# Normalising the probabilities before their transposes, and converting weights in steps of 512 columns, in a fused top-k attention and rational FFN kernel

## The chip, the cores and the metric

The kernel runs on one core of one Trainium2 chip. The core has five engines that work from queues of their own: TensorE (PE in the profile, with its weight loads shown apart as PEld), VectorE (DVE), ScalarE (ACT), GpSimd (POOL) and SyncE (SP), which here only issues transfers. Each engine executes its instructions in the order in which they stand in its queue, and waits on semaphores for the others. The metric is the device time of one execution in microseconds (us), as a median over runs.

## The reference

Eight batches of eight heads with 576 positions of 64 numbers go through attention that keeps the 32 largest scores of each row. Its output, 4608 tokens of 512 numbers, goes through an FFN whose activation is a ratio of two polynomials.

```python
scores = scale * np.matmul(q, k.transpose(0, 1, 3, 2))
kth = np.partition(scores, -top_k, axis=-1)[..., -top_k:-top_k + 1]
scores = np.where(scores >= kth, scores, -1000000000.0)
attn = np.exp(scores - np.max(scores, axis=-1, keepdims=True))
attn = attn / (np.sum(attn, axis=-1, keepdims=True) + 1e-09)
x = np.matmul(attn, v)        # then laid out as 4608 x 512
...
h = x @ w_in
P = a[0] + a[1] * h + a[2] * h2 + a[3] * h3
Q = 1.0 + np.abs(b[0]) * np.abs(h) + np.abs(b[1]) * h2
g = P / (Q + 1e-06)
return (g @ w_out).astype(np.float32)
```

The weights `w_in` (512 x 2048) and `w_out` (2048 x 512) arrive as 64-bit floats and are turned into 32-bit ones on the chip.

## The kernel before

A **tile** is 128 queries of one head against all 576 keys; there are 288, counted with the tiles of the last 64 queries, for which two heads share one tile (such a unit is called `mixed`). Two tiles, the two heads `h` of a head pair `hp`, make a **unit** (160 of them, 32 of which are mixed). Four head pairs times two units of queries fill a **chunk** of 256 tokens, and there are 18 chunks.

One tile (`add_tile`) goes through these steps. PE computes the scores `s` into PSUM. ACT copies them to `sb`. DVE folds the two halves of a row into `hi` and `lo`, and then finds the 32nd largest by MAX8 and MATCH_REPLACE8 in turns (tiles `m`, `hi`, `lo`). ACT makes the exponentials `e`, for which POOL or ACT has scaled the row's largest score to `st`. DVE multiplies `e` by the mask into `pr` and adds up the row into `ss` (L791). `pr` has two buffers of one unit each.

One unit (`add_values`) then goes on: POOL or ACT adds 1e-9 to the sums (`guard`), DVE takes the reciprocal (`inverse`, L846), and ACT widens the reciprocals of both heads to a 128 x 128 tile `rw` (`widen`, L285). PE transposes the probabilities in three parts, 4, 4 and 1 blocks of 128 columns, into PSUM tiles `trp` (L868), and with the third part also `rw` (L870). ACT copies each part to `p` (L880); the third part has 256 columns, half of them the transposed reciprocals. After both units of a pair PE multiplies `p` by the values into `av` (L894), ACT copies `av` to the chunk's tile `x` or `xm` (L911, L921), and POOL multiplies that by the transposed reciprocals (L913, L925). So the division by the sum stands at the end, on 64 output columns per head.

The **FFN** of a chunk works in 8 groups of 256 hidden columns (`add_group`). PE computes `ph` in 24 matmuls (L1041, three products of a split into high and low parts). ACT computes three functions of `ph`, POOL the cubic (L1115, L1116), ACT three functions more, POOL the ratio (L1097), its rounded part `g` (L281) and the rest `gl` (L1103), and PE adds the group's share into `po` in 12 matmuls (L1187). There are 144 groups. The working tiles of a group are taken from a pool `t` of 14 tiles of 512 columns. The PSUM tag `mm` with two banks is shared by `trp`, `ph` and `av`.

**Weights** are converted in the first 200 us, in 32 blocks of 128 x 512 and each block in two steps of 256 columns: two functions on ACT (L416, L421), a merge on DVE (L427), one more function on ACT (L433) and a product on POOL (L437).

The **order** is made at build time by `Plan`. Each step has a key, a list of engines that may run it, and modelled lengths; a list scheduler walks through a modelled time, and on a free engine starts the ready step with the lowest key whose buffers are free. What it decides is written out as the fixed order of each engine's queue. The numbers of the keys are in `KEY`. `STAY` is taken off the key of a PE step of the kind (ordinary or rounded 32-bit operands) that PE has just run; before it is 0. At the end of the program PE writes one row `flag_row` that DVE reduces (L1337), which decides whether a second, exact version of the program is run; in the profiled execution it isn't.

## Time and profile before

| | us |
|---|---|
| median of 3 runs | 1486.34 |
| lowest and highest | 1482.77 and 1486.7 |
| the profiled execution, its own time | 1483.46 |
| span of that execution, first to last instruction | 1481.4 |

The profile gives for each engine the time in which it was busy, groups of equal instructions with the mean length of one, and the waits with what ended them. A recorded length reaches from the start of an instruction to its end; on PE, DVE and ACT the next instruction often starts before that end, so the price of one instruction in a row of others is read from start to start. The profiled execution's span leaves 2.1 us of its own time outside, and its own time is 2.9 us under the median.

### The profile page before, as it was taken

The page shows a single profiled execution, that of the slowest core. Times are in us where ns is not written, and L with a number is a line of the kernel's source. Part 1 is how long each engine was busy: PE and PEld are TensorE (multiplying, and loading weights), DVE is VectorE, ACT ScalarE, POOL GpSimd, SP SyncE. Part 2 cuts the span into 40 slices and gives each one's busy share as a digit, 9 for nine tenths or more (in the row PEclk, how much of TensorE's full clock was granted, in tenths as well). Part 3 has the DMA queues.
Part 4 walks back from the last instruction along what each step waited for, and adds up shares of the span by engine and source line. Part 5 has one row for each costly group of instructions (what it writes and reads, how often), then busy time and mean ns, then how long its engine had stood idle before and what let it go on. Part 6 is the DMA issues. An engine that isn't in the chain of part 4 may idle for free.

```text
span 1481.4 us, 32234 instructions
## 1 busy us (share of the span) xinstructions
PE 1388.4 (94%) x9729; PEld 1178.2 (80%) x9729; DVE 1353.0 (91%) x4567; ACT 1297.7 (88%) x2616; POOL 1183.8 (80%) x1756
## 2 busy tenths in 40 slices
PE   5566689999999999999999999999999999999998
PEld 3335568888887888888888888888888788888896
DVE  7999999999999999999999999999999999999100
ACT  7888889989897898999899989999898798999774
POOL 5987897789776796879777887788777696887896
PEclk9766899999999999999999999999999999999999
DMA  7887876567765767577766776567665767554564
GB/s 238 266 248 229 245 213 193 184 199 229 225 193 147 242 203 223 174 213 228 224 181 198 219 246 186 183 198 230 212 192 157 246 187 223 177 183 142 172 197 139
DMA packets 172744, 302.94 MB, mean 204 GB/s; under 512 B 24209, under 2 KB 77969, under 8 KB 172561
## 3 DMA queue, kind: packets, MB, share of 16 engines
q1 hardware_dynamic: 172560, 300.79, 66.5%
q8 instruction: 79, 1.29, 0.4%
q14 instruction: 105, 0.85, 0.2%
HBM read 229.94 MB, written 18.87 MB: 168 GB/s over the span
## 4 chain that ended last, share of the span: by engine, by line
PE 80%; DVE 6%; ACT 5%; POOL 4%; DMA 2%; issue 2%; SPq 1%; POOLq 0%; DVEq 0%; ACTq 0%
PE ph_m L1041 23%; PE po_m L1187 21%; PE av L894 10%; PE s L720 8%; PE trp L868 8%; PE ph_t L1041 3%; PE po_t L1187 3%; DVE m L749 2%; DVE hi L757 2%; PE s L711 2%; ACT p L880 1%; DVE pr L791 1%; PE trp L870 1%; ACT sb L727 1%; POOL cf L484 1%
## 5 line engine op out<-in xcount | busy, mean ns | idle before, releaser
L749 DVE MAX8 m<-hi 128x8 f32<-128x288 f32 (+1 forms) x1152 | 498.6, 453 | 0.2
L757 DVE MATCH_REPLACE8 hi<-m,hi 128x288 f32<-128x288 f32 x864 | 380.8, 445 | 0.0
L1041 PE MATMUL ph_m<-xh_m,win_h 128*128 128x256 f32 x1024 | 304.4, 297 | 6.6 <-DMA win_l<-w_w 2.7
L1041 PE MATMUL ph_m<-xh_m,wi_m 128*128 128x256 f32 x1024 | 290.8, 284 | 0.6 <-DMA wi_m<-win_l 0.5
L1041 PE MATMUL ph_m<-xl_m,win_h 128*128 128x256 f32 x1024 | 289.9, 283 | 0.0
L880 ACT COPY p<-trp 128x512 f32<-128x512 f32 (+1 forms) x448 | 226.9, 513 | 31.7 <-PE trp L868 22.7
L868 PE MATMUL trp<-ident,pr 128*128 128x128 f32 x1312 | 222.3, 282 | 27.3 <-ACT p L880 16.0
L791 DVE SCALAR_TENSOR_TENSOR pr<-sb,m,e 128x576 f32<-128x576 f32 x288 | 230.3, 800 | 1.3 <-ACT e L788 0.9
L1097 POOL TENSOR_TENSOR pa_m<-pa_m,va_m 128x512 f32<-128x512 f32 x128 | 165.4, 1292 | 78.4 <-ACT va_m L1094 76.3
L727 ACT COPY sb<-s 128x576 f32<-128x576 f32 x288 | 184.4, 640 | 49.7 <-PE s L720 35.0
L788 ACT ACTIVATE e<-sb,st 128x576 f32<-128x576 f32 x288 | 217.0, 754 | 12.2 <-DVE pr L791 7.6
L1187 PE MATMUL po_m<-wout,g_m 128*128 128x512 f32 x512 | 217.9, 426 | 0.4 <-POOL fl L774 0.4
L868 PEld LDWEIGHTS trp<-ident,pr 128*128 128x128 f32 x1312 | 165.3, 145 | 56.8 <-ACT p L880 17.9
L1041 PEld LDWEIGHTS ph_m<-xh_m,win_h 128*128 128x128 f32 x1024 | 195.0, 190 | 15.6 <-ACT p L880 4.2
L1187 PE MATMUL po_m<-wl_m,g_m 128*128 128x512 f32 x512 | 203.0, 397 | 1.9 <-DMA wl_m<-wout_l 1.8
L1187 PE MATMUL po_m<-wout,gl_m 128*128 128x512 f32 x512 | 202.5, 396 | 0.1
L1041 PEld LDWEIGHTS ph_m<-xl_m,win_h 128*128 128x128 f32 x1024 | 195.3, 191 | 2.6
L1041 PEld LDWEIGHTS ph_m<-xh_m,wi_m 128*128 128x128 f32 x1024 | 194.6, 190 | 1.1 <-DMA wi_m<-win_l 1.0
L894 PE MATMUL av<-p,vm 128*64 128x256 f32 (+1 forms) x1920 | 186.7, 343 | 4.0 <-ACT p L880 3.8
L1116 POOL TENSOR_TENSOR pa_m<-pa_m,hh_m 128x512 f32<-128x512 f32 x128 | 165.3, 1291 | 16.0 <-ACT hh_m L1122 6.3
L1103 POOL TENSOR_TENSOR gl_m<-pa_m,g_m 128x512 fp32r<-128x512 f32 x128 | 165.8, 1295 | 6.8 <-PE po_t L1187 0.3
L894 PEld LDWEIGHTS av<-p,vm 128*64 128x64 f32 x1920 | 111.7, 142 | 72.3 <-issue 15.4
(121 smaller groups left out, 3204.4 us busy)
## 6 DMA issues: line engine op xcount, KB each, us to landing
wi_m<-win_l SPq DMA_DIRECT2D x128, 512.0 KB, 3.8
wl_m<-wout_l SPq DMA_DIRECT2D x256, 256.0 KB, 3.2
q<-qx SPq DMA_DIRECT2D x252, 128.0 KB, 2.7
vm<-in_v_dram SPq DMA_DIRECT2D x96, 320.0 KB, 3.1
km<-in_qk_dram SPq DMA_DIRECT2D x32, 352.0 KB, 3.6
kl<-in_qk_dram SPq DMA_DIRECT2D x32, 288.0 KB, 4.0
w_w<-in_moe_w_in_dram SPq DMA_DIRECT2D x32, 256.0 KB, 5.1
w_w<-in_moe_w_out_dram SPq DMA_DIRECT2D x32, 256.0 KB, 3.6
```

The lines of the kernel that those rows point to most:

```text
L727: nc.scalar.copy(t.sb, t.s[:, :, 0:HF])
L749: nc.vector.max(to, t.both if not full and o == 24 else getattr(t, src))
L757: nc.vector.match_replace(x, t.m[:, o : o + 8], x, NEG)
L788: nc.scalar.activation(t.e, t.sb, AF.Exp, scale=SCALE, bias=t.st)
L791: nc.vector.scalar_tensor_tensor(out=t.pr, in0=t.sb, scalar=t.kth, in1=t.e, op0=ALU.is_ge, op1=ALU.mult, accum_out=u.ss[:, t.h : t.h + 1],)
L868: nc.tensor.transpose(u.ps[i][:, c * P : (c + 1) * P], u.pr[:, x], ident)
L880: nc.scalar.copy(pair.pT[i][:, at].rearrange("p c n -> p (c n)"), u.ps[i][:, 0 : n * P])
L894: nc.tensor.matmul(pair.av[d, 0 : u.nq * len(pair.units)], lhs, x[:, 0, d] if u.mixed else x[:, 0] if lone else x, start=(c == 0), stop=(c ...
L1041: nc.tensor.matmul(y.ph[:, f * NT : (f + 1) * NT], w, z[:, c, :], start=(c == 0 and i == 0), stop=(c == HP - 1 and i == 2),)
L1097: engine().tensor_tensor(out=y.pa, in0=y.pa, in1=y.va, op=ALU.mult)
L1103: engine().tensor_tensor(out=tile_("gl", F32R), in0=y.pa, in1=y.g.bitcast(F32), op=ALU.subtract)
L1187: nc.tensor.matmul(o.po[i], z, w, start=(ff == 0 and n == 0), stop=(ff == NF - 1 and n == 2),)
```

## The change

Three things change, and the planner's numbers with them.

1. **The division moves.** `widen`, the transpose of `rw` and the two products on POOL after `av` are gone. In their place a step `normal(h)` for each of the unit's tiles multiplies the 576 probabilities of a row in `pr` by the reciprocal, on POOL or ACT as the planner finds (172 stand on POOL and 116 on ACT in the built order). The transposes now wait for these products and no longer for L791 alone. The third part of `p` has 128 columns in place of 256. ACT's copy of `av` into `x` or `xm` is now the last step.
2. **Weight conversion in one step of 512 columns** for each block: one load, and each of the five operations once per block in place of twice. A variant on DVE alone that was not in use is dropped.
3. **Working tiles of the FFN.** The pool of 14 tiles `t` becomes 4 tiles `t` and 5 tiles `tt` of double width; `hh` and `va` share one `tt`, `g` and `gl` another. The rounding of `g` (`RH`) may run on ACT as well as on POOL; 46 of 144 stand on ACT.

In the planner, a PE step of the kind that PE has just run has 10 or 15 taken off its key, and 14 of the other numbers in `KEY` differ (among them `MOE` and `PACE`, which place the FFN's steps among the tiles', from 125.2 to 157.9 and from 17.4 to 19.1, and `EX` for the exponentials from 14.4 to 25.7).

```diff
-        items = sorted(ready, key=lambda i: (i[0] - KEY['STAY'] * self.stays(e, i[2]), i[1]))
+        stay = KEY['STF'] if self.kind == "f" else KEY['STR']
+        items = sorted(ready, key=lambda i: (i[0] - stay * self.stays(e, i[2]), i[1]))
...
-            s1 = add("ACT", act_sb(256), sign, [ld], key + 1)
...
+            s1 = add("ACT", act_sb(512), sign, [ld], key + 1)
+            s2 = add("ACT", act(512, 1) + 0.04, ends, [ld], key + 1, take=[bits_hold])
+            s3 = add("DVE", 0.65, merge, [s1, s2], key + 1, later=KEY['ML'])
+            s4 = add("ACT", act_sb(512), size, [s3], key + 2, give=[bits_hold])
+            last = [add("POOL", pool_t(512), join, [s4], key + 2, give=hold if plain else [])]
...
-        def widen():
-            u.rw = buf("rw", [P, 2, D], F32, f"rw_{u.nm}")
-            ss = u.ss[:, 0:nr].unsqueeze(2)
-            scaled(u.rw, ss.broadcast_to([P, 2, D]), 1.0)
+        def normal(h):
+            def emit():
+                x = u.pr[:, h * S : (h + 1) * S]
+                scaled(x, x, u.ss[:, h : h + 1])
+            return emit
...
-                if i == 2:
-                    nc.tensor.transpose(
-                        u.ps[i][:, P : 2 * P], u.rw.rearrange("p h d -> p (h d)"), ident
-                    )
...
-                n = NJ if i < 2 else 2
+                n = NJ if i < 2 else 1
...
-        rw = add(one(P, 0, KEY['WD']), None, widen, [inv, prev.rw], key + KEY['URG'], take=[rwhold], give=[u.uhold])
+        norm = [
+            add({**one(S, 1, KEY['NR']), "POOL": 0.74} if "POOL" in KEY['NR'] else one(S, 1, KEY['NR']),
+                None, normal(h), [inv], key + KEY['URG'] + h, give=[u.uhold])
+            for h in range(nr)
+        ]
...
-            dep = [t1]
-            if i == 2:
-                dep += [rw, dbl]
+            dep = norm[0:1] if i == 0 else norm[1:2] if i == 1 else norm + [dbl]
...
-            c = add("ACT", act(n), lambda: scale(1), [m2] + u.chunk.parts[0:1], key + KEY['URG'], give=[avh])
-            u.done = add("POOL", pool_t(n), lambda: scale(2), [c], key + KEY['URG'], give=[thold[2]])
+            u.done = add("ACT", act(n), scale, [m2] + u.chunk.parts[0:1], key + KEY['URG'], give=[avh])
...
-        mm, th = Hold("mm"), {n: Hold("t") for n in ("h", "va", "hh", "pa", "g", "gl")}
+        mm, th = Hold("mm"), {n: Hold(t) for n, t in (("hv", "tt"), ("pa", "t"), ("gg", "tt"), ("h", "t"))}
```

The order of the queues shows the change at two places. The first is on PE in the middle of the program, where the third part of one unit's transposes stands (`trp_4_3_1`, from `pr_3_1`; `po` are matmuls of the FFN, `av` the product with the values, `s` the scores). Before:

```order
L1187 MATMUL po_m_2_1_12665<-wout_87,g_m_2_3_12625 128x512
L1187 MATMUL po_m_2_1_12665<-wout_87,gl_m_2_3_12643 128x512
L1187 MATMUL po_m_2_1_12665<-wl_m_2_3_1_12976,g_m_2_3_12625 128x512
L868 MATMUL trp_4_3_1_13114<-ident,pr_3_1_12895 128x128
L870 MATMUL trp_4_3_1_13114<-ident,rw_3_1_13106 128x128
L1187 MATMUL po_m_2_0_12654<-wout_88,g_m_2_4_12780 128x512
L1187 MATMUL po_m_2_0_12654<-wout_88,gl_m_2_4_12809 128x512
L1187 MATMUL po_m_2_0_12654<-wl_m_2_4_0_12994,g_m_2_4_12780 128x512
L894 MATMUL av_3_1_13132<-p_4_2_1_12911,vm_1_2_12564 64x256
```

Now:

```order
L1121 MATMUL po_m_2_0_11981<-wout_89,gg_m_2_4_12320 128x512 x2
L1121 MATMUL po_m_2_0_11981<-wl_m_2_4_1_12377,gg_m_2_4_12320 128x512
L818 MATMUL trp_4_3_1_12535<-ident,pr_3_1_12358 128x128 x4
L669 MATMUL s_3_2_1_12546<-kb_2_9920,q_2_2_11968 128x288 x4
L818 MATMUL trp_4_3_1_12556<-ident,pr_3_1_12358 128x128
L1121 MATMUL po_m_2_1_11990<-wout_89,gg_m_2_4_12320 128x512 x2
L1121 MATMUL po_m_2_1_11990<-wl_m_2_4_1_12377,gg_m_2_4_12320 128x512
L1121 MATMUL po_m_2_0_11981<-wout_90,gg_m_2_5_12457 128x512 x2
```

The transpose of `rw` has gone, the second and the third part have moved apart by one tile's scores, and the rest of the row is as it was.

The second is on POOL in the middle of the program (`fl` is a check of the 32 largest, `ss` the sums, `pa`, `g`, `gl`, `gg` and `hv` the FFN's, `st` the scaled largest score, `x_m` the chunk). Before:

```order
L281 TENSOR_SCALAR g_m_0_4_11682<-pa_m_0_4_11542 128x512
L774 TENSOR_TENSOR fl_10990<-hi_0_1_11483,m_0_1_11507 128x2
L1103 TENSOR_TENSOR gl_m_0_4_11691<-pa_m_0_4_11542,g_m_0_4_11682 128x512
L281 TENSOR_SCALAR ss_0_1_11570<-ss_0_1_11570 128x2
L913 TENSOR_TENSOR x_m_0_11702<-x_m_0_11702,p_4_0_0_11510 128x256
L1115 TENSOR_SCALAR pa_m_0_5_11680<-pa_m_0_5_11680,cf 128x512
L1116 TENSOR_TENSOR pa_m_0_5_11680<-pa_m_0_5_11680,hh_m_0_5_11687 128x512
L1097 TENSOR_TENSOR pa_m_0_5_11680<-pa_m_0_5_11680,va_m_0_5_11697 128x512
```

Now:

```order
L282 TENSOR_SCALAR ss_4_3_10656<-ss_4_3_10656 128x1
L282 TENSOR_SCALAR gg_m_0_1_10713<-pa_m_0_1_10509 128x512
L288 TENSOR_SCALAR st_0_0_10630<-m_0_0_10629 128x1
L1037 TENSOR_TENSOR gg_m_0_1_10713<-pa_m_0_1_10509,gg_m_0_1_10713 128x512
L288 TENSOR_SCALAR pr_4_3_10655<-pr_4_3_10655,ss_4_3_10656 128x576
L804 TENSOR_SCALAR pr_4_3_10655<-pr_4_3_10655 128x64
L1049 TENSOR_SCALAR pa_m_0_2_10785<-pa_m_0_2_10785,cf 128x512
L1050 TENSOR_TENSOR pa_m_0_2_10785<-pa_m_0_2_10785,hv_m_0_2_10798 128x512
L282 TENSOR_SCALAR ss_0_0_10738<-ss_0_0_10738 128x2
L723 TENSOR_TENSOR fl_10438<-hi_0_0_10572,m_0_0_10629 128x2
L288 TENSOR_SCALAR pr_0_0_10737<-pr_0_0_10737,ss_0_0_10738 128x576
```

The product on `x_m` has gone, and the products on `pr` with 576 columns now stand between the FFN's products. Of the 172 on POOL, 89 stand directly behind a product of two tensors of 512 columns or more. Of the 116 on ACT, 19 stand directly ahead of a copy of scores to `sb`.

In the whole order, 384 matmuls `ph` and 243 matmuls `po` stood behind the last scores on PE before; now 384 and 228 do.

## Rows read from the trace of the kernel before

**Rows 1.** The page: busy time by engine; then DVE in 40 slices of the span.

```profile
PE 1388.4 (94%) x9729; PEld 1178.2 (80%) x9729; DVE 1353.0 (91%) x4567; ACT 1297.7 (88%) x2616; POOL 1183.8 (80%) x1756
...
DVE  7999999999999999999999999999999999999100
```

**Rows 2.** Busy time in three stretches: PE, PEld, DVE, ACT, POOL, PE's clock, DMA.

```profile
0.00:300.00 300.00, 222.05 (x1377) 173.70 (x1378) 285.40 (x959) 261.28 (x600) 242.60 (x416) 0.86 0.74 226
300.00:1376.00 1076.00, 1068.23 (x7754) 918.27 (x7753) 1066.89 (x3605) 970.07 (x1908) 857.39 (x1260) 1.00 0.66 202
1376.00:1481.00 105.00, 98.12 (x602) 86.26 (x600) 0.69 (x5) 66.37 (x110) 83.85 (x82) 0.98 0.54 169
```

**Rows 3.** Waits of DVE: total us, times, longest.

```profile
DVE again L1337 <- PE flag_row L1335: 97.9, 1, 97.9
DVE hi L738 <- ACT sb L727: 12.5, 12, 7.2
```

**Rows 4.** Timeline of PE near 804 us: start, length.

```profile
804.35 0.27 PE L868 MATMUL trp<-ident,pr 128*128 128x128 f32 x1
804.46 0.27 PE L870 MATMUL trp<-ident,rw 128*128 128x128 f32 x1
```

**Rows 5.** The chain that ended last: start, length, what, count.

```profile
1412.19 6.98 PE po_m L1187 x30
...
1443.17 2.88 PE ph_m L1041 x24
```

**Rows 6.** Groups by form on PE: count, busy us, mean ns, idle before.

```profile
L870 PE MATMUL trp<-ident,rw 128*128 128x128 f32 x160 | 44.8, 280 | 6.5 <-ACT rw L285 5.6 <-DMA w_w<-in_moe_w_out_dram 0.9
```

**Rows 7.** Groups by form on ACT.

```profile
L788 ACT ACTIVATE e<-sb,st 128x576 f32<-128x576 f32 x288 | 217.0, 754 | 12.2 <-DVE pr L791 7.6 <-POOL st L287 2.3 <-POOL qx L281 1.0
...
L880 ACT COPY p<-trp 128x512 f32<-128x512 f32 x288 | 166.7, 587 | 23.8 <-PE trp L868 22.7
...
L880 ACT COPY p<-trp 128x256 f32<-128x256 f32 x160 | 60.8, 380 | 7.9 <-PE trp L870 6.5 <-POOL xm L925 0.7
L285 ACT ACTIVATE rw<-ss 128x128 f32<-128x128 f32 x160 | 50.5, 315 | 5.4 <-DVE ss L846 4.5 <-PE trp L870 0.3
L421 ACT ACTIVATE w_w_b<-w_w,toggle 128x256 f32<-128x256 uint32 x64 | 31.4, 503 | 0.3
...
L279 ACT ACTIVATE kh<-kl 128x576 fp32r<-128x576 f32 x5 | 3.4, 677 | 0.0
```

**Rows 8.** Groups by form on POOL.

```profile
L1097 POOL TENSOR_TENSOR pa_m<-pa_m,va_m 128x512 f32<-128x512 f32 x128 | 165.4, 1292 | 78.4 <-ACT va_m L1094 76.3
...
L281 POOL TENSOR_SCALAR g_m<-pa_m 128x512 fp32r<-128x512 f32 x128 | 79.5, 621 | 6.3
L913 POOL TENSOR_TENSOR x_m<-x_m,p 128x256 f32<-128x256 f32 x64 | 47.3, 739 | 7.5 <-ACT x_m L911 7.4
...
L925 POOL TENSOR_TENSOR xm<-xm,p 64x64 f32<-64x64 f32 x64 | 20.4, 319 | 12.8 <-ACT xm L921 9.6 <-DVE pr L791 0.5
...
L281 POOL TENSOR_SCALAR kh<-kl 128x576 fp32r<-128x576 f32 x27 | 18.2, 674 | 3.0 <-DMA kl<-in_qk_dram 1.7 <-issue 1.0
```

**Rows 9.** Timeline of DVE near 167 us, a step of weight conversion.

```profile
167.02 0.43 DVE L427 SCALAR_TENSOR_TENSOR w_w_b<-w_w,w_w_b 128x256 int32<-128x256 int32 x1 [0.75 <-ACT w_w_b L421]
167.35 0.08 DVE L757 MATCH_VALUE_LOAD hi<-m,hi 128x8 f32 x1
167.43 0.44 DVE L757 MATCH_REPLACE8 hi<-m,hi 128x288 f32<-128x288 f32 x1
167.79 0.45 DVE L738 TENSOR_TENSOR hi<-s,sb 128x288 f32<-128x288 f32 x1
```

**Rows 10.** Timeline of DVE near the last units.

```profile
1366.92 0.80 DVE L791 SCALAR_TENSOR_TENSOR pr<-sb,m,e 128x576 f32<-128x576 f32 x1
...
1370.31 0.16 DVE L846 RECIPROCAL ss<-ss 128x2 f32<-128x2 f32 x1
```

**Rows 11.** Timeline of PE at the same place.

```profile
1368.03 0.60 PE L868 MATMUL trp<-ident,pr 128*128 128x128 f32 x4
```

More of the change, by code (lines that the diff above doesn't have):

```diff
@@ L361, in load @@
             def load():
-                o.raw = []
-                for i, e in enumerate(range(0, 512, 256)):
-                    x = words(i)
-                    if i == 0:
-                        o.first = x
-                    r = x.bitcast(I32)
-                    nc.sync.dma_start(r, rows[:, e : e + 256].bitcast(I32))
-                    r = r.rearrange("p (e t) -> p e t", t=2)
-                    o.raw.append((slice(e, e + 256), r[:, :, 0], r[:, :, 1], x[:, 0:256]))
-                o.w = hi if plain else words(2)
@@ new lines, in load, with place_bits @@
+                o.first = words(0)
+                r = o.first.bitcast(I32)
+                nc.sync.dma_start(r, rows.bitcast(I32))
+                r = r.rearrange("p (e t) -> p e t", t=2)
+                o.raw = r[:, :, 0], r[:, :, 1]
+                o.w = hi if plain else words(1)[:, 0:512]
+                o.low = o.first[:, 0:512].bitcast(F32R) if away is not None else lo
+            ld = add("SP", dma(1, P * 1024), load, key=key, take=hold)
+            bits_hold = Hold(bank_tag)
+            def place_bits():
+                o.bits = bank(bits_hold, [P, 512], f"w_{nm}_b").bitcast(I32)
+                return o.bits
@@ new lines, in sign, with ends, merge, size @@
+            def sign():
+                nc.scalar.activation(o.w, o.raw[1].bitcast(F32), AF.Sign)
+            def ends():
+                nc.scalar.activation(
+                    place_bits().bitcast(F32), o.raw[0].bitcast(U32), AF.Identity, scale=THREE, bias=toggle
+                )
+            def merge():
+                nc.vector.scalar_tensor_tensor(
+                    o.bits, o.raw[1], 3, o.bits, op0=ALU.logical_shift_left, op1=ALU.bitwise_xor
+                )
+            def size():
+                nc.scalar.activation(o.first[:, 0:512], o.bits.bitcast(F32), AF.Abs)
@@ L899, in multiply, with scale @@
             return emit
-        def scale(part=0):
+        def scale():
             x = u.chunk
@@ L909, in scale @@
                 av = pair.av[:, 0 : n * P].rearrange("p (j n) -> p j n", j=n)
-                if part == 1:
-                    nc.scalar.copy(y, av)
-                elif part == 2:
-                    nc.gpsimd.tensor_tensor(out=y, in0=y, in1=rb[:, 0:n], op=ALU.mult)
-                else:
-                    nc.vector.tensor_tensor(y, av, rb[:, 0:n], ALU.mult)
+                nc.scalar.copy(y, av)
                 return
@@ L918, in scale @@
                 u.batch.xm = buf("xm", [P, HP, TAIL], F32, f"xm_{u.bi}")
-            y = u.batch.xm[:, u.hp]
-            if part == 1:
-                nc.scalar.copy(y, pair.av[:, 0:TAIL])
-                return
-            for h in range(2):
-                d = slice(h * D, (h + 1) * D)
-                nc.gpsimd.tensor_tensor(out=y[d], in0=y[d], in1=rb[d, 0, d], op=ALU.mult)
+            nc.scalar.copy(u.batch.xm[:, u.hp], pair.av[:, 0:TAIL])
         def put():
@@ L1128, in add_group @@
         wdep = []
-        held = [th[n] for n in (("hh", "va", "pa", "h") if full else ("hh", "va", "pa"))]
+        held = [th[n] for n in (("hv", "pa", "h") if full else ("hv", "pa"))]
         early = not full and x.n < KEY['TN']
@@ L1163, in add_group @@
         l2 = add("ACT", act_sb(512), inverse, [l1], k2 + 0.7)
-        gg = add(two(512, *KEY['ratio']), None, ratio, [l2, s3], k2 + 0.8, give=[th["va"]])
-        used = [th["g"], th["gl"]] if split_g else [th["pa"]]
+        gg = add(two(512, *KEY['ratio']), None, ratio, [l2, s3], k2 + 0.8, give=[th["hv"]])
+        used = [th["gg"]] if split_g else [th["pa"]]
         for h in used:
@@ L1168, in add_group @@
         if split_g:
-            gg = add(one(512, 0, KEY['RH']), None, ratio_high, [gg], k2 + 0.8, take=[th["g"]])
+            gg = add(one(512, 0, KEY['RH']), None, ratio_high, [gg], k2 + 0.8, take=[th["gg"]])
             gg = add(two(512, *KEY['ratio_low']), None, ratio_low, [gg], k2 + 0.8,
-                     take=[th["gl"]], give=[th["pa"]])
+                     give=[th["pa"]])
         def project(f, i):
```

119 lines of the change are left out of this document (28 added, 91 removed).

## The prediction, made before the changed kernel was run

> **What bounds the kernel now.** I read four views, in this order.
>
> First the busy time by engine and the slices [rows 1]. PE is the fullest engine, with 94% of the span, and DVE has 91%. But the slices of DVE show how its share comes about: it is full from the first slice on and stops altogether three slices before the end. So the program has two stages, and a share over the whole span mixes them.
>
> Second the busy time of stretches [rows 2]. From 300 to 1376 us DVE is busy for 1066.9 of 1076 us and PE for 1068.2. Both are full; ACT has 90% and POOL 80% of this stretch. From 0 to 300 us DVE is busy for 285.4 of 300 and PE for 222. From 1376 us on DVE has nothing left, and PE works for 98.1 of 105 us on the FFN of the last chunks. The granted clock is 1.00 in the middle stretch, the 2.4 GHz level.
>
> Third the waits of DVE [rows 3]. The largest, 97.9 us, is the last one, for the row that PE writes at the end. It is the length of the second stage. The largest before that is 12.5 us for copied scores, of which 7.2 us are the very first tile. Busy time and these gaps give the first stage as 7.2 us at the start, about 1352 us of work (1353.0 less the last few instructions), and some 16 us of gaps, altogether 1376.
>
> So the time is this sum: **DVE's work, plus DVE's gaps, plus what PE has left when DVE is done.** PE sets the pace of the first stage only as far as DVE would be waiting for it, and DVE's gaps are all that could be won there.
>
> **The change part by part.** The sum is made against the profiled execution's own 1483.46 us.
>
> *The 160 transposes of `rw` leave PE.* A recorded one is 0.28 us long [rows 6], but it starts 0.11 us after the transpose before it [rows 4], and that is what it holds up the next. 160 x 0.11 = 17.6 us of PE's time. All but the last few lie in the first stage, where DVE is as full as PE, so they don't shorten it by themselves. They give PE room. What fills it stands in the order: behind the last scores PE had 243 matmuls `po` and now has 228, with 384 `ph` in both. 15 matmuls at 6.98/30 = 0.233 us [rows 5] are 3.5 us that have moved from the second stage into the first, and two of the removed transposes stood in the second too. The second stage gets **3.7 us shorter**. The other 14 us become idle time of PE.
>
> The Trainium skill, "TensorE: Matmul & The Clock Gate", Part 4 on PE-mode transpose, gives about 275 ns for a 128 x 128 transpose within a kernel. The recorded length agrees with it; by it the removal would be worth an estimated 160 x 0.275 = 44 us of PE. The starts in the trace say 0.11 us, and these I take.
>
> *DVE's own work.* The selection and the masks are the same instructions. Only the merges of weights change: 64 of 256 columns become 32 of 512. A merge holds DVE for 0.33 us, and an instruction over 288 columns for 0.36 [rows 9]: 32 columns cost 0.03, so 0.06 of the 0.33 are fixed and one of 512 columns takes about 0.60. 64 x 0.33 - 32 x 0.60 = **1.9 us less**; with nothing fixed it would be 0, with half of it fixed 5.
>
> *ACT.* Off it go 160 widenings of 0.315 us, 50 us, and half of the columns of 160 copies: (587 - 380) / 256 = 0.81 ns a column, 160 x 128 x 0.81 = 17 us [rows 7]. Of the three functions in weight conversion the longest takes 503 ns for 256 columns; 64 x 0.503 - 32 x (0.503 + 0.207) = 9.5 us less, and I take 20 for the three. On it come 116 normalisations of 576 columns, at 0.68 us as for a plain one to 0.75 as for one with a scalar read from a tile [rows 7], so 79 to 87 us, and 46 roundings of 512 columns at no more than 0.68, 31 us. Net 23 to 31 us more on 1298.
>
> *POOL.* Off it go the products at the end, 47.3 + 20.4 us, and 46 roundings of 0.621, 29 us; on it come 172 normalisations of 0.67 to 0.75 us [rows 8], 115 to 129 us. Net 18 to 32 us more on 1184; about 82% of the span.
>
> Neither bounds anything by its sum. What matters is whether PE and DVE come to wait for them. Before, the first transpose of a unit started 0.3 us after its mask was made (the mask starts at 1366.92 and takes 0.8 [rows 10], the transpose starts at 1368.03 [rows 11]). Now it waits for the reciprocal, which starts at 1370.31, 2.6 us behind the mask, and then for a product of 0.7 us: some 3.5 us later, the second head's up to 4.3. What is queued behind it on PE waits too, if the order has it too early; the order was made with these lengths, and the example shows the third part moved behind a tile's scores. The buffer `pr` is held by that much longer. There are two, and a unit takes DVE two tiles of 1352 / 288 = 4.7 us each, so the unit after next needs one at about 9.4 us: the cover is about 5 us wide. When the last unit is done the delay lies beside some 37 us of other chunks' `ph`, 13 groups of 2.88 us [rows 5].
>
> A copy of scores that stands behind a normalisation on ACT comes up to 0.75 us later, and DVE's folds wait for those copies. There are 19 such places, 14 us at the most. Before, such copies stood behind a widening of 0.315 us in 63 places, which go: 20 us at the most. So DVE's gaps have reason to shrink a little, the more as PE is freer to make scores early. I take **2.5 us less**, between 9 less (all gaps of the middle stretch, 1076 - 1066.9) and 14 more.
>
> *Weight loads* become half as many of twice the size; DVE is the limit in that stretch, and they lie beside it. I cost them at nothing.
>
> *Sum:* 1.9 + 3.7 + 2.5 = 8.1 us less. 1483.46 - 8.1 = 1475.4; the median of the runs lies 2.9 us above the profiled execution, which gives **1478.2 us**.
>
> The Trainium skill, "GPSIMD Engine Reference", in its opening, calls GpSimd the wrong choice for ordinary elementwise arithmetic, where VectorE is about twice as fast. That speaks against this change. By that page, as an estimate, 288 products on DVE at half of 0.67 us would put 97 us onto the sum, since DVE is full in the first stage and POOL is not [rows 2]; the rows speak against the rule here.
>
> **The rivals.**
>
> *PE was the one that set the pace.* Then the 17.6 us count in full: 1486.3 - 17.6 - 1.9 = 1467. For it: both engines are full in the same stretch, and most of DVE's gaps are waits for scores. Against it: DVE's gaps in that stretch are 9.1 us, so it can't follow PE by more. If a transpose cost its whole recorded length, 0.28 us, this would be 44.8 us and 1440; that figure is the one of the skill's page, and the starts in the trace exclude it.
>
> *Nothing arrives.* The change does what it says on PE, but the room becomes idle time, and new waits of ACT for `p` take up the few us elsewhere: 1486. For it: the FFN stands at the same place of the order but for 15 matmuls, so little can move.
>
> *PE waits for POOL.* Of the 172 normalisations on POOL 89 stand directly behind a product of two tensors, such as L1097 of 1.29 us [rows 8]. If POOL is late at such a place, transposes come late and PE, in order, stands with all that is behind it, scores for DVE among it. One in four, 22 x 1.29 = 28 us, less the 17.6 us of room, is 11 us: 1497. It decides from the 14th such place on, where the room is used up. Against it: POOL has 20% of idle time in the middle stretch.
>
> **How the numbers follow.** Forecast, DVE keeps its pace (1470 to 1484): 0.57. PE in full: 0.11, and 0.01 of it for 1440. Nothing arrives: 0.17. PE waits for POOL: 0.15. The range leaves out half of the slower case and a part of the fast one: 1467 to 1495. 0.3%, about 4.5 us, is what a measurement of this kernel can tell from no change. Of the forecast's 0.57 about 0.46 lie beyond it on the fast side and 0.11 within; with PE in full that is 0.57 faster. Within: 0.11 + 0.15 of the third case = 0.26. Slower: 0.15 + 0.02 = 0.17.
>
> **What would show it.** Right: DVE's last wait is about 94 us in place of 97.9, DVE's busy time about 2 to 5 us less, its gaps no larger, L870 and L285's `rw` gone, and PE's busy share in the middle stretch down to about 98%. Wrong: PE waits for POOL's or ACT's `pr` of tens of us (the third rival), DVE's folds waiting for `sb` more than 20 us (ACT is late), or DVE full and yet done much earlier (then its work was not what I took for the bound).

## The result, and the profile after

| | before | after |
|---|---|---|
| median of 6 runs each, us | 1485.09 | 1492.69 |
| lowest and highest | 1482.77, 1486.7 | 1491.24, 1497.15 |
| the profiled execution: own time, span | 1483.46, 1481.4 | 1492.58, 1490.8 |

The ratio is 1.0053, with a 95% interval of 1.0041 to 1.0065. The change makes the kernel slower by 0.5%, where the forecast said 1478.2 and faster; the time lies within the range of 1467 to 1495.

The page of the kernel after, busy time by engine and DVE in 40 slices, answers [rows 1]:

```profile
PE 1384.6 (93%) x9569; PEld 1157.7 (78%) x9569; DVE 1355.2 (91%) x4535; ACT 1320.4 (89%) x2534; POOL 1212.2 (81%) x1710
...
DVE  7999999999999999999999999999999999999200
```

ACT is 22.7 us busier and POOL 28.4, about as worked out (23 to 31 and 18 to 32). The groups by form show the new instructions and what became of [rows 7] and [rows 8]:

```profile
L288 POOL TENSOR_SCALAR pr<-pr,ss 128x576 f32<-128x576 f32 x172 | 128.7, 751 | 15.0 <-DVE ss L795 13.5 <-PE s L669 1.1
L286 ACT ACTIVATE pr<-pr,ss 128x576 f32<-128x576 f32 x116 | 89.9, 784 | 0.5 <-DVE ss L795 0.5
L826 ACT COPY p<-trp 128x128 f32<-128x128 f32 x160 | 45.6, 285 | 1.0 <-PE trp L818 0.8
```

The windows of the kernel after (PE, PEld, DVE, ACT, POOL, PE's clock, DMA) answer [rows 2] and show where the time went:

```profile
0.00:300.00 300.00, 220.59 (x1316) 168.11 (x1318) 280.97 (x912) 253.51 (x491) 244.56 (x381) 0.85 0.74 226
300.00:1376.00 1076.00, 1056.45 (x7574) 895.74 (x7571) 1062.30 (x3584) 985.31 (x1906) 874.62 (x1239) 1.00 0.66 200
1376.00:1491.00 115.00, 107.57 (x683) 93.81 (x681) 11.98 (x41) 81.61 (x139) 93.02 (x92) 0.98 0.54 169
```

Up to 1376 us DVE stands still for 300 - 280.97 + 1076 - 1062.30 = **32.7 us**, where it stood still for 14.6 + 9.1 = 23.7 before. It still has 11.98 us of work behind that point, where it had 0.69. So the first stage ends some 12 us later: 9.0 us of new idle time, half of it in each of the two stretches, a last wait of 1.1 us at its end, and 2.2 us of longer busy time. The clock in the middle is 1.00 as before.

The waits of the kernel after (total, times, longest) answer [rows 3], with those of PE for the new products:

```profile
DVE again L1271 <- PE flag_row L1269: 94.6, 1, 94.6
DVE hi L687 <- ACT sb L676: 18.4, 23, 7.0
PEld trp L818 <- POOL pr L288: 14.0, 21, 2.4
PE trp L818 <- POOL pr L288: 7.2, 8, 1.7
```

The second stage is 3.3 us shorter. DVE's folds wait 23 times for copied scores in place of 12. And there is a wait that the kernel before didn't have: the transposes for GpSimd's products (PEld loads `pr` for PE, so that the two rows overlap).

### The profile page after: what moved, and what is told of

Its sections match the earlier page's. It is cut to its first block, busy times and chain, and to the rows that moved or that the text cites. A ratio compares the mean times of both kernels' runs of the same rounds, so it can differ in the third digit from the quotient of the medians.

```text
span 1490.8 us, 31684 instructions
## 1 busy us (share of the span) xinstructions
PE 1384.6 (93%) x9569; PEld 1157.7 (78%) x9569; DVE 1355.2 (91%) x4535; ACT 1320.4 (89%) x2534; POOL 1212.2 (81%) x1710
## 4 chain that ended last, share of the span: by engine, by line
PE 65%; DVE 12%; POOL 8%; ACT 7%; DMA 4%; issue 3%; SPq 1%; POOLq 0%; ACTq 0%; DVEq 0%
PE ph_m L968 19%; PE po_m L1121 17%; PE av L840 9%; PE s L669 7%; PE trp L818 6%; DVE m L698 3%; DVE hi L706 3%; PE ph_t L968 3%; PE po_t L1121 3%; DVE pr L740 2%; DMA wi_m<-win_l 2%; ACT sb L676 2%; PE s L660 1%; ACT p L826 1%; DVE hi L687 1%
## 5 line engine op out<-in xcount | busy, mean ns | idle before, releaser
L1121 PE MATMUL po_m<-wout,gg_m 128*128 128x512 f32 x1024 | 338.4, 411 | 1.5 <-POOL gg_m L1037 1.2
L826 ACT COPY p<-trp 128x512 f32<-128x512 f32 (+1 forms) x448 | 210.3, 484 | 24.1 <-PE trp L818 23.4
L1031 POOL TENSOR_TENSOR pa_m<-pa_m,hv_m 128x512 f32<-128x512 f32 x128 | 166.0, 1297 | 54.2 <-ACT hv_m L1028 53.5
L968 PEld LDWEIGHTS ph_m<-xh_m,win_h 128*128 128x128 f32 x1024 | 194.6, 190 | 19.1 <-ACT p L826 6.8
L1121 PE MATMUL po_m<-wl_m,gg_m 128*128 128x512 f32 x512 | 202.0, 395 | 0.0
L1121 PEld LDWEIGHTS po_m<-wout,gg_m 128*128 128x128 f32 x1024 | 172.2, 189 | 29.0 <-issue 3.2
L1050 POOL TENSOR_TENSOR pa_m<-pa_m,hv_m 128x512 f32<-128x512 f32 x128 | 165.6, 1294 | 20.9 <-ACT hv_m L1056 8.9
L1037 POOL TENSOR_TENSOR gg_m<-pa_m,gg_m 128x512 fp32r<-128x512 f32 x128 | 165.8, 1295 | 10.2 <-ACT gg_m L280 6.4
```

The source lines that it names most:

```text
L826: nc.scalar.copy(pair.pT[i][:, at].rearrange("p c n -> p (c n)"), u.ps[i][:, 0 : n * P])
L968: nc.tensor.matmul(y.ph[:, f * NT : (f + 1) * NT], w, z[:, c, :], start=(c == 0 and i == 0), stop=(c == HP - 1 and i == 2),)
L1031: engine().tensor_tensor(out=y.pa, in0=y.pa, in1=y.va, op=ALU.mult)
L1037: engine().tensor_tensor(out=tile_("gl", F32R), in0=y.pa, in1=y.g.bitcast(F32), op=ALU.subtract)
L1121: nc.tensor.matmul(o.po[i], z, w, start=(ff == 0 and n == 0), stop=(ff == NF - 1 and n == 2),)
```

## The experiments

**The theories.** A: the length of the normalisations delays the transposes, and what stands behind them on PE, scores for DVE among it, comes late; A2 is its half on GpSimd, the other half being those on ScalarE ahead of copies of scores. B: the weight steps of 512 columns hold DVE up. C: the order differs, by its new numbers or by accident, and neither part costs by itself.

### The normalisations shortened or doubled in the order of the kernel after

```diff
 x = u.pr[:, h * S : (h + 1) * S]
+x = x[:, 64:128]                                          # e1: all 288
+x = x[:, 64:128] if plan.at == "ACT" else x               # e2: the 116 on ScalarE
+x = x[:, 64:128] if plan.at == "POOL" else x              # e3: the 172 on GpSimd
+x = x[:, 64:384] if plan.at == "POOL" else x              # e3h
 scaled(x, x, u.ss[:, h : h + 1])
+if plan.at == "POOL":                                     # doubled
+    nc.gpsimd.tensor_scalar(x, x, 1.0, 0.0, op0=ALU.mult, op1=ALU.add)
```

Each run has one of the added pieces; e1 to e3h leave most of the affected probabilities undivided, and only their times are read. The order of all queues is that of the kernel after, word for word, but for the second product in the last one.

> The changed kernel in its own order, but each normalisation works on 64 of its 576 columns (so most probabilities stay undivided): same instructions, same waits, each some 0.4 us shorter on ScalarE and 0.5 us on GpSimd. Theory A (the length of the 288 products, in queues that feed VectorE's folds and TensorE's transposes, makes the gaps of VectorE): VectorE's first stage ends near 1376 us in place of 1386.9, and the time falls by 8 to 11 us, to 1482 to 1485. Theory B (the steps of 512 columns in weight conversion): nothing changes, 1491 to 1494, since the loss is in the first 210 us for another reason. Theory C (the planner's numbers gave an order that is worse by itself): between 0 and 4 us of gain, the gaps stay.

> The changed kernel in its own order, but the 116 normalisations on ScalarE work on 64 of 576 columns (those rows stay undivided elsewhere), the 172 on GpSimd whole. Shortening all 288 gave 1482.3 us. Theory A1 (the loss is on ScalarE, where the copies of scores stand): nearly all of the 10 us comes back, 1482 to 1486, and VectorE's gaps behind copies with ScalarE full fall from 4.9 to about 2.5 us. Theory A2 (the loss is on GpSimd, whose products delay scaled maxima and transposes): 1488 to 1492.

> The changed kernel in its own order, but the 172 normalisations on GpSimd work on 64 of 576 columns, the 116 on ScalarE whole. Theory A1: little comes back, 1489 to 1493. Theory A2: most of the 10 us, 1482 to 1486. If both this and the run with ScalarE's shortened give about half, each engine's queue delays the other's work.

> The changed kernel in its own order, with the 172 normalisations on GpSimd on 320 of the 576 columns (256 columns of each row stay undivided in these tiles). From 64 to 576 columns the time rose by 8.3 us, from 576 to 1152 by 60.8. If each column costs the same up to 576, this run lies in the middle, 1488 to 1489. If the price begins at some length, where the room is used up, it lies near the run with 64 columns, 1484 to 1486.

> The changed kernel in its own order, but behind each of the 172 normalisations on GpSimd stands one more instruction of the same size on the same 576 columns, which multiplies by 1 and adds 0. The order of all other instructions is untouched. It adds 172 x 0.72 us = 124 us to GpSimd, and each transpose waits 0.72 us longer. Theory A2 (the loss is the length of the normalisations on GpSimd; shortening them to 64 columns gave back 8.3 us): a second dose costs at least as much as the first, 8 us and more, so 1501 us or above, and since GpSimd then has only some 70 us of idle time left in the first stage, the price should be far above 8 us, 1510 to 1560; DVE's gaps grow, and TensorE's waits for pr from GpSimd grow from 21 us (PE and PEld together, in which the two overlap) to over 50. Rival (the order was upset by something else, and the products on GpSimd lie in idle time): within 3 us of the changed kernel, 1490 to 1496.

"Idle" is DVE's up to 1376 us, worked out from the two first windows of each run as above; PE and PEld are their waits for GpSimd's `pr`, `sb` those of DVE's folds into `hi` for copied scores, and "GpSimd" those of DVE's own waits (over 0.15 us, up to 1376 us) that end with a result of GpSimd. Each ratio is to the kernel before on the same chip as the run; those medians of the kernel before lie between 1484.84 and 1486.22 us.

| columns on GpSimd, on ScalarE | median | ratio to before, 95% | idle | PE, PEld | `sb` | GpSimd |
|---|---|---|---|---|---|---|
| 64, 64 (e1) | 1482.31 | 0.9979 (0.9969 to 0.9990) | 24.5 | 1.9, 4.3 | 15.2 | 2.3 |
| 64, 576 (e3) | 1484.44 | 0.9985 (0.9975 to 0.9995) | 25.7 | 2.3, 4.5 | 15.5 | 1.9 |
| 320, 576 (e3h) | 1486.93 | 1.0014 (1.0002 to 1.0026) | 29.8 | 3.8, 8.0 | 17.0 | 3.7 |
| 576, 64 (e2) | 1490.69 | 1.0034 (1.0021 to 1.0047) | 32.1 | 9.0, 15.7 | 16.8 | 6.2 |
| 576, 576 (after) | 1492.69 | 1.0053 (1.0041 to 1.0065) | 32.7 | 7.2, 14.0 | 18.4 | 5.3 |
| twice 576, 576 | 1553.48 | 1.0445 (1.0428 to 1.0463) | 85.0 | 43.7, 63.3 | 49.9 | 22.3 |

With GpSimd's products short, the same order is at the kernel before's time, and DVE's idle time and the wait for `pr` go with it. By the medians the 172 products on GpSimd account for 8.3 of the 10.4 us that all 288 give back, the 116 on ScalarE for 2.0; by the ratios it is 10.1 of 11.0 and 2.8, and the interval of e2 overlaps that of the kernel after. Theories B and C fall with e1: order, steps and numbers are those of the kernel after there, and the loss is gone. What is left then is the 3.3 us of the second stage: DVE's idle time, 24.5, is the kernel before's 23.7, and the time is 0.2% below.

Between 64 and 576 columns the price rises about evenly: halfway between 0.9985 and 1.0053 lies 1.0019, and the run with 320 columns, 1.0014, agrees with that and excludes the time at 64, though its median, 1486.93, lies between the two ranges that were expected. From 64 to 576 columns GpSimd is busy for 73 us more and the time is 8.3 us longer; from 576 columns to twice as many it is 60.8 us for 110 us, some five times as much for each microsecond of work. The windows of that run:

```profile
0.00:300.00 300.00, 213.71 (x1254) 163.60 (x1255) 272.99 (x881) 244.38 (x473) 254.52 (x399) 0.82 0.71 220
300.00:1376.00 1076.00, 1025.18 (x7217) 858.38 (x7217) 1018.01 (x3417) 941.20 (x1815) 920.32 (x1318) 0.99 0.64 194
```

GpSimd is busy for 920.32 of 1076 us there. It still idles for 14.5% of the stretch, and yet DVE stands still for 58.0 us of it.

**The chain at one place.** One and the same fold of DVE, in the same order, in two of these runs. First the kernel after, from its timeline (start, length; in brackets the idle time just before and what ended it):

```profile
867.19 0.15 DVE L795 RECIPROCAL ss<-ss 128x2 f32<-128x2 f32 x1
...
868.13 1.45 POOL L546 TENSOR_TENSOR kl<-kl,kh 128x576 fp32r<-128x576 f32 x1
...
869.55 0.75 POOL L288 TENSOR_SCALAR pr<-pr,ss 128x576 f32<-128x576 f32 x1
...
870.36 0.66 PE L818 MATMUL trp<-ident,pr 128*128 128x128 f32 x4 [0.87 <-POOL pr L288]
...
870.95 1.30 POOL L1031 TENSOR_TENSOR pa_m<-pa_m,hv_m 128x512 f32<-128x512 f32 x1
...
872.29 0.63 ACT L280 ACTIVATE gg_m<-pa_m 128x512 fp32r<-128x512 f32 x1 [0.65 <-POOL pa_m L1031]
...
872.62 0.77 PE L669 MATMUL s<-kb,q 128*128 128x288 f32 x4
...
872.97 0.79 DVE L740 SCALAR_TENSOR_TENSOR pr<-sb,m,e 128x576 f32<-128x576 f32 x1
...
873.96 0.64 ACT L676 COPY sb<-s 128x576 f32<-128x576 f32 x1
...
874.63 0.46 DVE L687 TENSOR_TENSOR hi<-s,sb 128x288 f32<-128x288 f32 x1 [0.50 <-ACT sb L676]
```

The reciprocal is there at 867.34, but GpSimd is in other work until 869.58, of which the last 1.45 us is a product of two tensors. Its normalisation ends at 870.30. Two engines wait for what comes late from GpSimd here: PE 0.87 us for the normalised `pr`, and ScalarE 0.65 us for the FFN's ratio (L1031), which stands behind the normalisation in GpSimd's queue. The same place with 64 columns on GpSimd (e3):

```profile
859.79 0.16 DVE L795 RECIPROCAL ss<-ss 128x2 f32<-128x2 f32 x1
...
861.39 0.33 POOL L288 TENSOR_SCALAR pr<-pr,ss 128x64 f32<-128x64 f32 x1
...
861.80 0.62 PE L819 MATMUL trp<-ident,pr 128*128 128x128 f32 x4
...
863.70 0.63 ACT L280 ACTIVATE gg_m<-pa_m 128x512 fp32r<-128x512 f32 x1 [0.51 <-POOL pa_m L1032]
...
864.03 0.78 PE L669 MATMUL s<-kb,q 128*128 128x288 f32 x4
...
865.37 0.64 ACT L676 COPY sb<-s 128x576 f32<-128x576 f32 x1
...
865.56 0.81 DVE L740 SCALAR_TENSOR_TENSOR pr<-sb,m,e 128x576 f32<-128x576 f32 x1
...
866.65 0.45 DVE L687 TENSOR_TENSOR hi<-s,sb 128x288 f32<-128x288 f32 x1
```

Here GpSimd starts the normalisation 1.44 us behind the reciprocal's end, not 2.21, and is done 0.42 us sooner. The copy ends at 866.01, and DVE comes to it 0.64 us later without a pause. That 0.64 us is all the cover that the place had. Against DVE's mask, which does not wait in either run, the transposes start 865.56 - 861.80 = 3.76 us ahead here and 872.97 - 870.36 = 2.61 us ahead in the kernel after: 1.15 us later. ScalarE's rounding `gg`, and the copy with it, are 1.18 us later. The cover takes 0.64 of that, and DVE's wait of 0.50 is about what is left.

Which of the two ways holds the copy up? It starts 1.67 us behind the rounding in both runs, while PE's scores are done some 0.57 us ahead of it, at 873.39 and 864.81. So ScalarE's queue sets the copy's start here. The fold is late because GpSimd's ratio is, and the rounding, one of the 46 that moved to ScalarE, waits for it. Had only PE been late, a copy started with the scores' end would by estimate have been done at 873.39 + 0.64 = 874.03, ahead of DVE, which is free at 874.13. In the run with 320 columns PE waits 0.35 us here and DVE not at all; in the doubled run DVE waits longest, and the copy, at 916.10, again starts 1.68 us behind the rounding:

```profile
912.49 0.66 PE L820 MATMUL trp<-ident,pr 128*128 128x128 f32 x4 [0.73 <-POOL pr L802]
...
914.42 0.63 ACT L280 ACTIVATE gg_m<-pa_m 128x512 fp32r<-128x512 f32 x1 [0.66 <-POOL pa_m L1033]
...
916.77 0.46 DVE L687 TENSOR_TENSOR hi<-s,sb 128x288 f32<-128x288 f32 x1 [0.99 <-ACT sb L676]
```

**Where the idle time comes from.** From e3 to the kernel after DVE's idle time grows by 7.0 us. Of these, 3.2 are waits of folds for copied scores, and 3.4 are waits of DVE for GpSimd's own results: the check `fl` and the FFN's coefficients `cf`, which stand behind the normalisations in GpSimd's queue. The kernel before, in its own order, has 5.4 us of the latter kind as well; with short products the new order is rid of most of them. DVE's waits up to 1376 us for `fl`, `flags` and the first coefficients, in e3 and in the kernel after:

```profile
DVE hi L687 <- POOL fl L723: 0.2, 1, 0.2
DVE cf L437 <- POOL cf L433: 0.2, 1, 0.2
```

```profile
DVE cf L437 <- POOL cf L433: 1.7, 3, 0.7
DVE hi L687 <- POOL fl L723: 1.3, 3, 0.7
DVE flags L640 <- POOL fl L723: 1.0, 1, 1.0
```

One such place in the kernel after, where e3 has no pause: the fold may write `hi` only when GpSimd's check has read what stood there.

```profile
1059.98 0.74 POOL L288 TENSOR_SCALAR pr<-pr,ss 128x576 f32<-128x576 f32 x1
...
1060.69 0.19 POOL L723 TENSOR_TENSOR fl<-hi,m 128x1 f32<-128x1 f32 x1
...
1060.91 0.46 DVE L687 TENSOR_TENSOR hi<-s,sb 128x288 f32<-128x288 f32 x1 [0.31 <-POOL fl L723]
```

Followed back over 12 us by what ended each wait, none of the 41 pauses of DVE over 0.15 us in the kernel after (up to 1376 us) leads to a wait of PE for GpSimd's `pr`; in the doubled run 37 of its pauses do, 31 us of its 85. So at the single dose A is right in that the length of GpSimd's products costs, but its way, by late transposes, is not what the trace shows. The price is set at each place by the lateness of whatever waits behind the normalisations there against the cover there.

### Steps of 256 columns, nudged orders, exchanged numbers

```diff
-add("ACT", act_sb(512), sign, ...)                # e4: each of the five operations in two halves
+for i in range(2): add("ACT", act_sb(256), sign, ...)
...
-'LOOK': 0.564    +'LOOK': 0.58                    # n1, on after
-'LOOK': 0.541    +'LOOK': 0.56                    # n2, on before
```

e5 is the kernel after with the 14 numbers of the kernel before and no preference for the kind that PE has just run; e6 is the kernel before with the 14 new numbers and the preference.

> The changed kernel with weight conversion back in two steps of 256 columns per block, the rest and the planner's numbers as changed. Theory A: within 3 us of 1492.7, and VectorE's gaps up to 300 us stay near 11 us. Theory B: the gaps up to 300 us fall from 11 to about 7 us and the time by 3 to 5 us, to 1488 to 1490. Theory C: a move of some us in either direction, since the planner makes a new order.

> The changed kernel with one number of the planner moved by 3% (LOOK from 0.564 to 0.58), which exchanges some tens of instructions with their neighbours and changes nothing else. Theory A: within 2 us of 1492.7. Theory C (the time hangs on the accidents of one order): a move of 3 us or more.

> The kernel before with the same number moved by 3.5% (LOOK from 0.541 to 0.56). Theory A: within 2 us of 1485. Theory C: a move of 3 us or more.

> The changed kernel's steps with the planner's 14 numbers of the kernel before, and no preference of TensorE for the kind it has just run. Theory A: still slow, 1490 to 1500, with VectorE's gaps at 25 us or more. Theory C: the time comes back to 1480 to 1486. If it is much slower than 1500, the new numbers were what the new steps needed.

> The kernel before with the 14 changed numbers and the preference for the kind that TensorE has just run, its steps as they were. Theory A: the time stays within 4 us of 1485, because the steps are what counts. Theory C: it becomes slower by 5 to 10 us, 1490 to 1495, with VectorE's gaps near 25 us.

Steps of 256 in the kernel after: 1497.58, ratio 1.0081 (1.0066 to 1.0096). The steps of 512 are 4 to 5 us better there, and B falls a second time. A's "within 3 us" missed as well; a move of that size is what C allowed for a new order, and whether the steps save the time or the numbers fit them is not told apart. The nudges gave 1493.36 and 1486.62, with ratios of 1.0046 (1.0032 to 1.0060) and 1.0005 (0.9994 to 1.0017): within 1 us of the kernels that they nudge. But exchanging all the numbers is no small thing: e5 took 1513.33 (1.0190), e6 1499.62 (1.0096), both outside the ranges of A and of C; by what was expected of e5, a time far over 1500 says that the new steps needed the new numbers. Each set of numbers fits its own kernel. In e5 the waits for GpSimd's products were the largest of all in which each is issued once, and the last wait of DVE was 10 us longer:

```profile
DVE again L1271 <- PE flag_row L1269: 104.7, 1, 104.7
...
PEld trp L818 <- POOL pr L288: 17.5, 15, 6.3
PE trp L818 <- POOL pr L288: 13.3, 7, 6.1
```

### The transposes put later

```diff
-x = add("PE", n * pe_t, transpose(i), dep, kk, ...)
+x = add("PE", n * pe_t, transpose(i), dep, kk, ..., later=1.0)      # l05: 0.5
```

> The changed kernel, but the order gives the transposes a place as if they could start 1 us later than the normalisations end, so that TensorE has something else in front of them where GpSimd is late. Theory A2 with in-order waiting as the mechanism: TensorE's waits for pr (7.2 us on PE, 14.0 on PEld) fall to a third, and the first stage gets back 3 to 8 us: 1484 to 1490. Rival (it is not the waiting of TensorE but the longer way from mask to transposed probabilities that costs, through buffers held for longer): no gain or a loss, 1492 to 1500, although the waits for pr fall.

> As the run before it with 0.5 us in place of 1. In-order waiting: between the changed kernel and the run with 1 us, 1486 to 1491. Longer way through held buffers: at 1492 to 1496. If the two doses do not stand in order with the changed kernel, the difference is that of one order against another and tells nothing on either.

Measured: 1496.07 with 1 us, 1.0060 (1.0044 to 1.0075); 1489.51 with half of it, 1.0026 (1.0016 to 1.0036). The first lies in the rival's range, the second in that of in-order waiting. PE's and PEld's waits for `pr`, 7.2 and 14.0 us in the kernel after, were 4.4 and 6.2 with 1 us, less but not a third, and 7.8 and 10.0 with half, where PE's did not fall. The times don't stand in order with the dose, so by the expectation they tell nothing for or against A. With 1 us DVE's folds waited 25.0 us for `sb`, more than in the kernel after: taking the wait off PE's queue by moving the transposes did not take it off DVE. This one is inconclusive.

### The division put back, the rest kept

```diff
-norm = [add(one(S, 1, KEY['NR']), None, normal(h), [inv], ...) for h in range(nr)]
+rw = add(one(P, 0, KEY['WD']), None, widen, [inv, prev.rw], ...)    # and L870, L913, L925 of before
...
-'RH': ('ACT', 'POOL')    +'RH': ('POOL',)                            # d2p, d1p, p2
-'RH': ('POOL',)          +'RH': ('ACT', 'POOL')                      # b_round, on before
```

Two theories more were tried here for what the rest of the change costs by itself: R, that the rounding of `g` on ScalarE makes copies of scores late, and N, that a set of numbers fits one set of steps only (T is B with the working tiles added).

> The other half of the change alone: weight conversion in steps of 512 columns and the working tiles of double width, with the kernel before's division at the end (widening, transposed reciprocals, products on the output), its planner numbers and no preference for the kind. Theory A2 (the loss is in the normalisations): no loss, 1480 to 1487 against 1485, with DVE's merges 2 to 5 us cheaper and PE's waits for weights about as before. Rival (the steps of 512 columns or the scarcer working tiles hold the first stage up): 1490 and more, with DVE's gaps before 300 us over 10 us.

> Division at the end and the planner's numbers as in the kernel before, weight conversion in steps of 512 columns, working tiles of double width, and the rounding of g on GpSimd alone, as before. Against d2_steps_512_alone (1496.0) only the rounding moves. Theory R (the rounding on ScalarE makes copies of scores late): DVE's waits for sb fall from 23.6 us to about 13, and the time falls to 1481 to 1487. Theory T (steps or tiles): 1490 to 1500, with DVE's gaps as in d2_steps_512_alone, about 30 us. Theory N (the numbers don't fit the other lengths): anything within 10 us, with no one kind of gap that goes.

> The kernel before with one thing changed: the rounding of g may run on ScalarE or on GpSimd, as the planner finds. Theory R: slower by 5 us or more, 1490 to 1500, with DVE's waits for sb above 18 us (12.5 before). Theories T and N: T says within 3 us of 1486; N says slower by an amount that is not bound to the waits for sb.

> The changed kernel with the rounding of g on GpSimd alone. GpSimd gets 46 x 0.62 = 29 us more and ScalarE 31 us less. Theory A2 (length and place of work on GpSimd ahead of the transposes): slower than the changed kernel, 1496 to 1510, with larger waits of TensorE for pr from GpSimd. Theory R (the rounding on ScalarE costs): faster than the changed kernel, 1480 to 1490.

> The changed kernel with the division alone undone: widening, transposed reciprocals and products on the output as before, everything else and the planner's new numbers as after. Theory A2 alone: faster than the changed kernel by about 8 us, 1482 to 1488. Theory N (the numbers fit one set of steps and no other): slower than the changed kernel, 1494 to 1515, as the new numbers cost the kernel before 14 us.

> The division at the end as before, the rest of the change with its numbers, and the rounding of g on GpSimd alone as before. Against d1_division_undone (1487.6): taking the rounding off ScalarE cost nothing measurable with the old numbers and 6 us with the normalisations on GpSimd. If it is GpSimd's lateness ahead of the transposes that costs, nothing on GpSimd stands there here but the sums, and the time stays within 3 us of 1487.6; if the rounding on ScalarE is what d1 loses against the kernel before, 1482 to 1485, faster than both kernels.

| division | steps, tiles | numbers | rounding | median | ratio, 95% |
|---|---|---|---|---|---|
| end | before | old | GpSimd | before | 1 |
| end | before | old | either (b_round) | 1489.32 | 1.0022 (1.0010 to 1.0034) |
| end | before | new | GpSimd (e6) | 1499.62 | 1.0096 (1.0081 to 1.0112) |
| end | after | old | either (d2) | 1496.01 | 1.0066 (1.0053 to 1.0079) |
| end | after | old | GpSimd (d2p) | 1497.26 | 1.0078 (1.0055 to 1.0100) |
| end | after | new | either (d1) | 1487.60 | 1.0018 (1.0005 to 1.0030) |
| end | after | new | GpSimd (d1p) | **1483.86** | 0.9984 (0.9971 to 0.9996) |
| ahead | after | old | either (e5) | 1513.33 | 1.0190 (1.0172 to 1.0207) |
| ahead | after | new | either (after) | 1492.69 | 1.0053 (1.0041 to 1.0065) |
| ahead | after | new | GpSimd (p2) | 1498.82 | 1.0094 (1.0075 to 1.0113) |

Three comparisons change the division alone, in orders that the planner makes anew: by 1492.69 - 1487.60 = 5 us with the rounding on either engine, 1498.82 - 1483.86 = 15 us with the rounding on GpSimd, and 1513.33 - 1496.01 = 17 us with the old numbers (5, 16 and 18 by the ratios). **The division ahead of the transposes is slower in all three**, and by more where GpSimd has the roundings as well. d1 came out at the upper end of A's 1482 to 1488 and below N's 1494 to 1515; d2 missed A's 1480 to 1487 and lies in its rival's range, and d2p missed R's 1481 to 1487.

With the division at the end, the new steps with the new numbers take 1487.60 and 1483.86; with the old numbers they take 1496.01 and 1497.26, and the old steps with the new numbers 1499.62. So N holds between the numbers on one side and steps and tiles on the other: either one without the other costs 10 to 14 us. Which of the new steps and tiles needs the new numbers was not tried. R is no answer for the change as a whole: the rounding on ScalarE costs 3 to 5 us in b_round and d1, nothing in d2, and gains 6 in the kernel after. In d1p the time came as expected for the case that the rounding is what d1 loses against the kernel before. For p2 the time came as A2 said, but not the way: the waits for `pr` were no larger (6.2 and 12.8), and 3.1 us of its loss lie in the second stage, whose wait is 97.7 us.

d1p is the fastest version that computes everything, 0.16% below the kernel before with an interval that ends just under 1; that is within the 0.3% that a measurement of this kernel can tell from no change.

## Why the prediction was wrong, by its own steps

- **What bounds the kernel: right.** DVE's work, DVE's gaps and the second stage make up the whole difference. The profiled span grew by 9.4 us; 9.0 and 1.1 of idle time plus 2.2 of busy time less 3.3 of the second stage make 9.0.
- **Second stage, 3.7 us less: right.** It measured 3.3.
- **PE's room: right, and worth nothing.** PE's busy share from 300 to 1376 us is 1056.45 / 1076 = 98.2%, as forecast.
- **ACT and POOL: right** in their sums (22.7 and 28.4 us more). A normalisation measured 0.75 us on GpSimd, the upper bound, and 0.78 on ScalarE, just above it.
- **DVE's own work, 1.9 us less: right for the merges, and covered up by the rest.** A merge of 512 columns holds DVE for 0.61 us, against a forecast of 0.60, and 64 x 0.33 - 32 x 0.61 makes 1.6 us:

```profile
170.33 0.69 DVE L382 SCALAR_TENSOR_TENSOR w_w_b<-w_w,w_w_b 128x512 int32<-128x512 int32 x1 [1.03 <-ACT w_w_b L377]
170.94 0.08 DVE L706 MATCH_VALUE_LOAD hi<-m,hi 128x8 f32 x1
```

  All the same, busy time rose by 2.2 us to 1355.2. With the normalisations short it is 1352.8, and in d1p, which has the same merges, 1350.6. The last section shows what interruptions add; what they leave of the rise is not accounted for.
- **DVE's gaps, 2.5 us less with a range from 9 less to 14 more: this is the step that failed.** They came out 9.0 us more. It counted copies of scores on ScalarE that no longer stand behind a widening, and treated ScalarE as the engine to watch; ScalarE's normalisations cost 2 to 3 us, GpSimd's 8 to 10. Of GpSimd's normalisations it asked only what the later `pr` does to PE and to the buffer `pr`, whose cover of 5 us did hold: DVE has no wait for it. It did not ask what 172 products of 0.75 us do to that which stands behind them in GpSimd's own queue. DVE waits for the checks and coefficients there, ScalarE's roundings for the ratios, and copies of scores stand behind the roundings. At the place shown the cover was 0.64 us.
- **The argument against the third rival, that POOL idles for 20% of the stretch: wrong.** A share of idle time says nothing on whether the engine is free in the microsecond when the reciprocal comes. In the kernel after GpSimd still idles for 19%, and in the doubled run for 14.5% while DVE loses 58 us.
- **The third rival had the right engine, but not the way nor the condition.** It is GpSimd, late behind a product of two tensors, and PE does stand in order behind it. But that was to cost only from the 14th place on, when PE's 17.6 us of room are used up. PE's waits for `pr` came to 7.2 us in 8 places, with PEld's to 14.0 in 21, less than the room, and the time was lost all the same, by what else waits for GpSimd. In the doubled run, where PE waits 43.7 us, a part of DVE's pauses does lead back to PE. PE's free time elsewhere gives back nothing of a pause that DVE has made.

The Trainium skill, "GPSIMD Engine Reference", in its opening, calls GpSimd the wrong engine for plain elementwise arithmetic; the prediction set that aside because the same products on DVE would cost more. The runs agree that these products on GpSimd cost time. The page's reason, that VectorE is faster, is not what they show: what cost was the place of the work in GpSimd's queue and its length there, and the products on DVE were not tried.

## What to carry to other kernels

A step that is put into the middle of a chain is not paid for by the idle share of the engine that gets it: ask what stands in front of it in that engine's queue when its operand comes, what stands behind it there and behind its consumer, who waits for each of these, and how early the bounding engine's next operand would have been ready. Shortening the new step in the unchanged order, and doubling it, tells its price from that of the order in two runs. And where a planner's numbers were chosen together with a set of steps, undoing one of the two alone measures the misfit.

## What the runs showed of the hardware

**Interruptions make DVE's busy time longer.** The same 4535 instructions, with mean lengths of the long ones within 1% of each other, were busy for 1352.8 us in e1, 1355.2 in the kernel after and 1362.4 in the doubled run:

```profile
PE 1376.0 (93%) x9569; PEld 1156.6 (78%) x9569; DVE 1352.8 (91%) x4535; ACT 1278.4 (86%) x2534; POOL 1136.1 (77%) x1710
```

```profile
PE 1407.0 (91%) x9569; PEld 1167.6 (75%) x9569; DVE 1362.4 (88%) x4535; ACT 1324.0 (85%) x2534; POOL 1322.4 (85%) x1882
```

Instructions in a row overlap: in [rows 9] the fold at 167.79 starts 0.08 us before the end of the one ahead of it. One that waits for its operand loses that beside the pause itself. The doubled run has 97 pauses where e1 has none. At these places the time from start to start, less the pause, is 8.1 us longer in all than in e1, 0.08 us each; that is most of the 9.6 us.

**GpSimd's load did not lengthen DVE's mask.** The Trainium skill, "GPSIMD Engine Reference", section 1, Specifications, says that GpSimd shares its interfaces to the on-chip memory with VectorE and contends with DVE instructions that read two inputs there. That would have been another cause of a late DVE. The mask, which reads `sb` and `e`, doesn't show it, in the kernel after and in the doubled run:

```profile
L740 DVE SCALAR_TENSOR_TENSOR pr<-sb,m,e 128x576 f32<-128x576 f32 x288 | 230.3, 800 | 3.3 <-ACT e L737 2.5
```

```profile
L740 DVE SCALAR_TENSOR_TENSOR pr<-sb,m,e 128x576 f32<-128x576 f32 x288 | 230.7, 801 | 7.1 <-ACT e L737 6.5
```

800 ns and 801 ns, with 110 us more of GpSimd's busy time in the second. For this instruction the cost was in the waiting, not in its length.
